# Gated linear attention ahead of two MLPs: the attention of chunks 9 to 23 in 64x64 quadrants, one visit a chunk

## The chip, the cores and the metric

The kernel runs on one core of one Trainium2 chip, in a single launch. The metric is the device time of that core in microseconds (us), smaller is better. PE is the matmul engine, DVE the vector engine, ACT the scalar (activation) engine, POOL the general-purpose engine, SP the engine that issues most DMAs. Each engine works through its own list of instructions in order and waits on semaphores.

## The reference, cut to what matters

```python
def _attn_ref(q, k, v, alpha):            # batch 4, heads 8, seq 768, head_dim 48
    state = np.zeros((B, H, D, D), dtype=np.float32)
    for t in range(S):
        state = alpha[:, :, t, :, None] * state + np.einsum('bhd,bhe->bhde', k[:, :, t], v[:, :, t])
        y[:, :, t] = np.einsum('bhd,bhde->bhe', q[:, :, t], state)
# x: y as 3072 tokens x 384
# MLP 1: h = x @ w_in (384 x 2048); g = h * sigmoid(h); x = g @ w_out
# MLP 2: sigmoid(x @ w_gate) * (x @ w_val), both 384 x 1536; then @ w_out
```

Everything is float32 outside; the weights reach the kernel as 64-bit words that it converts.

## The kernel before

**Chunks.** The 3072 tokens are 24 chunks of 128 (`C`), six to a sequence. Eight heads are four pairs (`NP`); the two heads of a pair lie on partitions 0 to 47 and 64 to 111 (`j` = 0, 1). Inside a chunk the recurrence becomes matrix products: `prep` (L278) scans the decays forward (A) and backward (G) on DVE, multiplies the keys by G and the queries by A, and leaves the decay over the whole chunk in `AE`.

**A chunk's products.** `scores` (L310) transposes the keys (PE, L319) and forms, for each head, the 128x128 block of keys times queries (L323) in two PSUM banks. `scores_done` masks the block with the causal triangle on DVE (L334, one instruction of 1024 columns, into M), and copies the transposed keys on ACT. `results` (L341) multiplies values by M (L352), keys by values into the new part of the state (L368, `u`), and the old state by the queries (L373, into the same bank as the values' product). `state` (L382) adds `u` and multiplies by the decay on DVE (L388, L389). `y_out` copies the result on ACT and moves 16 rows of each head's half by DMA, since 3 x 128 partitions hold 8 x 48 rows; `x_out` rounds it to the high half and DVE forms the low half that MLP 1 needs.

**MLPs.** Tokens go in six blocks of 512. A float32 product is three fp32r matmuls of 128x128 weights by 512 columns (`mm3`, L565 to L567: high by low, high by high, low by high). A step is one block `b` and one 128-row slice `f` of the hidden layer: `mm_in` (9 matmuls), `act` on ACT and DVE, and `mm_out` (9 matmuls) for the slice of two steps earlier. A step is 18 matmuls on PE.

**Order.** It is written out by hand (`manual_schedule`). A lead does chunks 0 to 8, with `full` products one after the other (L722 to L741); it prepares chunk c+2 in pass c, so that chunk 9 is prepared there too. Then the steps of MLP 1 run: 28 of them (`mixed`) alternate blocks 0 and 1 and also convert weights (`Way.half`, on DVE, ACT and POOL: L479 to L522). The tables `SCORES`, `RESULTS` and `DECAYS` (L47 to L53) put the attention of chunks 9 to 23 into steps: place 0 is between `mm_in` and `mm_out`, place 1 behind `mm_out`, place 3 is preparation. So PE visits a chunk twice, once for the scores and once for the results. Block 0's sums occupy the PSUM group 0 until step (0, 15) is done; after that attention has this group. MLP 2 follows behind block 5.

**Queues.** SP issues in this order: after the scores of chunk c the keys and decays of chunk c+4 (`load_decays`), after its results the queries and values of c+4, then the row moves of `y_out`. Four places hold the chunks' q, k and alpha in turn. In the lead ACT issues half of the row moves.

```python
            h = early.pop((b, f), None) or mm_in(ps_h, "h", "in", b, f)
            tensor(i, 0)
            way = way1 if i < mixed else way2 if b == NB - 1 else None
            act(b, f, h, None, "out", way)
            others(i, 0)
            others(i, 3)
            if len(pend) > 2:
                mm_out()
            tensor(i, 1)
            others(i, 1)
```

Of the kernel before, what the change touches and what calls it, by code (L numbers as in the profile page):

```python
# [7 lines left out]
F32 = mybir.dt.float32  # L8
# [6 lines left out]
ALU = mybir.AluOpType  # L15
# [16 lines left out]
QW = 3 * NP * C  # L32
N = 512
# [148 lines left out]
def gated_attention_then_mlps(ctx: ExitStack, tc: tile.TileContext, qka, a0, v, w_in, w_out, w_gate, w_val, w_out2, out):  # L182
# [25 lines left out]
    causal = ap.tile([P, C], F32, name="causal")  # L208

    W = ap.tile([DP, NP * D + 16], F32, name="state")  # L210
    W_all = W[:, : NP * D].rearrange("r (p d) -> r p d", d=D)
# [31 lines left out]
    def constants():  # L243
# [5 lines left out]
        nc.gpsimd.affine_select(out=causal, in_=causal, compare_op=ALU.is_ge, fill=0.0, base=0, pattern=[[1, C]], channel_multiplier=-1)  # L249
        nc.vector.memset(dg, 0.0)  # L250
# [4 lines left out]
        nc.gpsimd.memset(W, 0.0)  # L255
# [17 lines left out]
    def check(c, i):  # L273

        x = (Gt, At)[i].pop(c)
        nc.scalar.activation(x, x, AF.Square, accum_out=chk[:DP, c, i : i + 1])

    def prep(c, step, p0=0, p1=NP, mul=None):  # L278
# [5 lines left out]
        if step == 0:  # L284
            if p0 == 0:
                Gt[c] = G_at[c % 2]
                At[c] = ap.tile([DP, NP * C], F32, tag="A", name="A", bufs=2)
# [11 lines left out]
        elif step == 1:  # L299
            nc.vector.tensor_tensor_scan(At[c][:, lo:hi], t[:, A_OFF + lo : A_OFF + hi], d1[:, lo:hi], 0.0, op0=ALU.mult, op1=ALU.add)  # L300
        else:
            q = t[:, lo:hi]
            mul.tensor_tensor(q, q, At[c][:, lo:hi], op=ALU.mult)

    S, T, M, KT, U, Y = {}, {}, {}, {}, {}, {}
# [4 lines left out]
    def scores(c, g, apart, p0=0, p1=NP):  # L310

        t = qk[c]
        if p0 == 0:
            S[c] = two_banks(g)
            if not last_of(c):
                T[c] = ps_h.tile([P, N], F32, tag="h", name="t") if apart else bank(g)
# [14 lines left out]
    def scores_done(c):  # L331
        for_all = causal.rearrange("s (j i t) -> s j i t", j=1, i=1).to_broadcast([P, 2, NP, C])
        M[c] = ap.tile([P, 2, NP, C], F32, tag="m", name="m", bufs=2)
        nc.vector.tensor_tensor(M[c], S[c].rearrange("s j (i t) -> s j i t", i=NP), for_all, op=ALU.mult)  # L334
# [6 lines left out]
    def results(c, g):  # L341
# [6 lines left out]
        for p in range(NP):  # L348
            for j, n in ((0, 64), (1, D)):
# [3 lines left out]
                    y[r : r + n, p * C : (p + 1) * C], v_c[:, h : h + n], M[c][:, j, p], start=p == 0, stop=first, skip_group_check=True  # L353
                )
        s = S.pop(c)
        if not last_of(c):
            u = ps_h.tile([P, N], F32, tag="h", name="u")[:DP] if c < LEAD else s[:DP, 0]
            U[c] = u[:, : NP * D]
            kt = KT.pop(c)
            sums = c < LEAD and not first  # L360
            if sums:
                for j, n in ((0, 64), (1, D)):
                    r = 64 * j
                    nc.tensor.matmul(u[r : r + n, : NP * D], ident[r : r + D, r : r + n], W[r : r + D, : NP * D], start=True, stop=False, skip_group_check=True)
            for p in range(NP):
                for j, n in ((0, 64), (1, D)):
                    r = 64 * j
                    nc.tensor.matmul(u[r : r + n, p * D : (p + 1) * D], kt[:, p, r : r + n], vt[c][:, 2 * p + j], start=not sums, stop=True, skip_group_check=True)  # L368
        if not first:
            for p in range(NP):  # L370
                for j, n in ((0, 64), (1, D)):
# [3 lines left out]
                        W[r : r + D, p * D : p * D + n],  # L375
# [6 lines left out]
    def state(c):  # L382

        u, w = U.pop(c), W[:, : NP * D]
        if c < LEAD or c % CB == 0:
            w = u
        else:
            nc.vector.tensor_tensor(w, u, w, op=ALU.add)  # L388
# [510 lines left out]
```

## Time and profile before

| | |
|---|---|
| Median of 3 runs | 976.45 us (974.56 to 976.94) |
| Profiled execution, its own time | 976.87 us |
| its span, first to last instruction | 974.8 us |
| mean granted TensorE clock | 0.987 |
| busy: PE, DVE, ACT, POOL | 98%, 46%, 39%, 10% |

A row of the timeline has the start in us from the span's start, the length in us, the engine and line, output<-inputs by the program's names, and how many instructions were merged (x16). In brackets stands idle time of the engine just before, and who ended it. Windows give busy time of each engine in a stretch. PE is the matmuls themselves, PEld the loading of their weights; matmuls are pipelined, so the distance of two starts, not the length of one, is what one costs. An fp32 matmul shows as two instructions.

### The profile page before, as it was taken

The numbers are of one execution on the slowest core, as the hardware profiler recorded it, in microseconds if no ns is written. First come the engines' busy times: TensorE is split into PE (matmuls) and PEld (weight loads), VectorE is DVE, ScalarE is ACT, GpSimd is POOL, SyncE is SP. The second block draws the span as 40 slices with busy tenths as digits, with TensorE's granted clock in tenths as the row PEclk, the third lists the DMA queues.
The fourth block names the chain that finished last, engine by engine and source line by source line (L and its number), as shares of the span: only waits on it lengthen the run. The fifth ranks groups of instructions, "written<-read, shape, count | busy, mean of one in ns | idle before, by whom it ended". The sixth has DMA issues, their size and how long they took to land.

```text
span 974.8 us, 12868 instructions
## 1 busy us (share of the span) xinstructions
PE 951.3 (98%) x5192; PEld 777.2 (80%) x5192; DVE 450.6 (46%) x640; ACT 381.9 (39%) x707; POOL 92.9 (10%) x105
## 2 busy tenths in 40 slices
PE   7879999999999999999999999999999999999997
PEld 5658887878888888888888888888888888888885
DVE  8777778644543434342766444443232222222221
ACT  3446666443334334333666344433222222221211
POOL 2223323100000000000221111110000000000000
PEclk8899999999999999999999999999999999999999
DMA  9753332130111210003332112001000000000001
GB/s 229 210 150 117 129 100 80 40 107 28 58 42 37 70 38 13 5 1 102 98 98 67 63 65 65 33 1 42 24 1 0 33 1 1 33 1 0 33 1 37
DMA packets 35348, 54.84 MB, mean 56 GB/s; under 512 B 3856, under 2 KB 24368, under 8 KB 35280
## 3 DMA queue, kind: packets, MB, share of 16 engines
q1 hardware_dynamic: 34512, 53.37, 17.9%
q8 instruction: 43, 0.70, 0.3%
q10 hardware_dynamic: 768, 0.56, 0.2%
q14 instruction: 25, 0.20, 0.1%
HBM read 48.02 MB, written 4.72 MB: 54 GB/s over the span
## 4 chain that ended last, share of the span: by engine, by line
PE 89%; DVE 3%; DMA 2%; ACT 2%; issue 1%; POOL 1%; SPq 0%; ACTq 0%; DVEq 0%
PE h L565 13%; PE h L567 13%; PE h L566 13%; PE s L565 6%; PE s L567 5%; PE s L566 5%; PE o L567 3%; PE o L565 3%; PE o L566 3%; PE v L565 3%; PE v L566 3%; PE v L567 3%; PE y L565 3%; PE y L567 3%; PE y L566 3%; PE s L323 2%
## 5 line engine op out<-in xcount | busy, mean ns | idle before, releaser
L565 PE MATMUL h<-x,w 128*128 128x512 f32 x582 | 228.0, 392 | 3.1 <-ACT w L504 1.7
L567 PE MATMUL h<-x,w 128*128 128x512 f32 x582 | 227.0, 390 | 0.8 <-POOL w L522 0.8
L566 PE MATMUL h<-x,w 128*128 128x512 f32 x582 | 227.0, 390 | 0.0
L593 DVE TENSOR_TENSOR gl<-g,gh 128x512 fp32r<-128x512 f32 x168 | 115.9, 690 | 194.9 <-ACT gh L592 194.2
L592 ACT ACTIVATE gh<-g 128x512 fp32r<-128x512 f32 x168 | 106.2, 632 | 157.0 <-DVE g L587 153.9
L565 PEld LDWEIGHTS h<-x,w 128*128 128x128 f32 x582 | 109.2, 188 | 28.0 <-ACT w L504 2.1
L567 PEld LDWEIGHTS h<-x,w 128*128 128x128 f32 x582 | 109.3, 188 | 25.0 <-POOL w L522 1.7
L566 PEld LDWEIGHTS h<-x,w 128*128 128x128 f32 x582 | 109.2, 188 | 22.8
L584 ACT ACTIVATE g<-h 128x512 f32<-128x512 f32 x96 | 57.0, 593 | 154.8 <-PE h L567 154.8
L587 DVE TENSOR_TENSOR g<-v,g 128x512 f32<-128x512 f32 x46 | 31.8, 692 | 178.7 <-PE v L567 178.7
L565 PE MATMUL s<-gl,w 128*128 128x512 f32 x240 | 96.5, 402 | 0.0
L586 ACT ACTIVATE g<-h 128x512 f32<-128x512 f32 x72 | 42.9, 596 | 132.6 <-PE h L567 132.6
L567 PE MATMUL s<-gh,w 128*128 128x512 f32 x240 | 93.7, 390 | 0.0
L566 PE MATMUL s<-gh,w 128*128 128x512 f32 x240 | 93.6, 390 | 0.0
L565 PE MATMUL o<-gl,w 128*128 128x512 f32 x144 | 56.1, 390 | 0.0
L567 PE MATMUL o<-gh,w 128*128 128x512 f32 x144 | 56.1, 390 | 0.0
L566 PE MATMUL o<-gh,w 128*128 128x512 f32 x144 | 56.1, 389 | 0.0
L522 POOL TENSOR_TENSOR w<-tmp,w 128x384 fp32r<-128x384 f32 x36 | 36.4, 1030 | 195.0 <-ACT w L504 195.0
L565 PEld LDWEIGHTS s<-gl,w 128*128 128x128 f32 x240 | 45.0, 187 | 12.4 <-issue 1.4
L587 DVE TENSOR_TENSOR g<-h,g 128x512 f32<-128x512 f32 x26 | 18.0, 692 | 79.3 <-PE h L567 79.3
L565 PE MATMUL v<-x,w 128*128 128x512 f32 x138 | 53.9, 391 | 0.0
L566 PE MATMUL v<-x,w 128*128 128x512 f32 x138 | 53.8, 390 | 0.0
(120 smaller groups left out, 1280.8 us busy)
## 6 DMA issues: line engine op xcount, KB each, us to landing
x<-in_moe_w_in SPq DMA_DIRECT2D x16, 384.0 KB, 3.6
x<-in_moe_w_out SPq DMA_DIRECT2D x16, 384.0 KB, 4.1
x<-in_qka SPq DMA_DIRECT2D x12, 448.0 KB, 4.2
qk<-in_qka SPq DMA_DIRECT2D x11, 448.0 KB, 3.7
v<-in_v SPq DMA_DIRECT2D x24, 192.0 KB, 3.1
raw<-in_moe_w_gate SPq DMA_DIRECT2D x12, 384.0 KB, 3.5
raw<-in_moe_w_val SPq DMA_DIRECT2D x12, 384.0 KB, 3.8
raw<-in_moe_w_out SPq DMA_DIRECT2D x12, 384.0 KB, 3.7
```

Source lines behind the costliest of these rows:

```text
L323: nc.tensor.matmul(S[c][:, j, p * C : (p + 1) * C], t[r : r + D, NP * C + p * C : NP * C + (p + 1) * C], t[r : r + D, p * C : (p + 1) * C] ...
L522: nc.gpsimd.tensor_tensor(l, b[:, i * SW : (i + 1) * SW].bitcast(F32), h.bitcast(F32), op=ALU.subtract)
L565: nc.tensor.matmul(ps, wh, x_l, start=first, stop=False)
L566: nc.tensor.matmul(ps, wh, x_h, start=False, stop=False)
L567: nc.tensor.matmul(ps, wl, x_h, start=False, stop=last)
L584: nc.scalar.activation(g, h, AF.Silu)
L586: nc.scalar.activation(g, h, AF.Sigmoid)
L587: nc.vector.tensor_tensor(g, val, g, op=ALU.mult)
L592: nc.scalar.activation(gh, g, AF.Copy)
L593: nc.vector.tensor_tensor(gl, g, gh.bitcast(F32), op=ALU.subtract)
```

## The change

For chunks 9 to 23 a chunk's 128 tokens are cut into two halves of 64 (`HC`). Only the two diagonal 64x64 blocks of the scores are formed; what the second half needs of the first goes through a state between them, so each chunk has two states (`W[c % 2][:, 0]` and `[:, 1]`). Every product uses 64 rows and up to 64 columns of the array: scores go to row half `j`, column half `h`; sums and values to row half `h`; the state's products to row half `j`, with the second half's outputs swapped (`j ^ h`). Bank `h` of one PSUM pair holds the results and the sums of half `h`. A `drain` of PE stands ahead of the state's products.

A chunk has one visit: transposes of chunk c+2, sums of c+1, values of c, scores of c+1, state's products of c. The tables `VISIT`, `G_AT` and `A_AT` place visits and preparation; chunk 9 is prepared in steps (0, 5) and (1, 5) and no longer in the lead. In the lead the mask multiply is two instructions of 512 columns, and M lies in weight buffers not yet in use. `tensor(i, 0)` is written behind `act`; the order of PE's own instructions stays. Last chunks of a sequence now have transposes and the sums of their first half. Left out below: renamed functions (`full_...`: the lead's), constants, and one-line tile changes.

```diff
-SCORES = {9: (1, 12, 0), 10: (1, 13, 0), 11: (1, 14, 0), 12: (1, 15, 2)}
-RESULTS = {9: (1, 12, 1), 10: (1, 13, 1), 11: (1, 14, 1), 12: (2, 2, 0)}
-
-DECAYS = {10: ((1, 9), (1, 10)), 11: ((1, 12), (1, 12)), 12: ((1, 14), (1, 14))}
-for _c in range(13, NC):
-    SCORES[_c] = (_c // 4 - 1, (0, 4, 8, 11)[_c % 4], 0)
-    RESULTS[_c] = (_c // 4 - 1, (2, 6, 10, 13)[_c % 4], 0)
+FIRST = {"T": (1, 11, 0), "scores": (1, 12, 0)}
+VISIT = {9: (1, 12, 1), 10: (1, 13, 0), 11: (1, 14, 0)}
+X_AT = {9: (1, 14)}
+G_AT = {9: (0, 5), 10: (0, 10), 11: (1, 9), 12: (1, 11), 13: (1, 13)}
+A_AT = {9: (1, 5), 10: (1, 8), 11: (1, 10), 12: (1, 12)}
+for _c in range(12, NC):
+    VISIT[_c] = (_c // 4 - 1, (2, 6, 10, 13)[_c % 4], 0)
...
+    def scores(c, p0=0, p1=NP):
+        t = qk[c]
+        if p0 == 0:
+            S[c] = bank(0), ps_h.tile([P, N], F32, tag="h", name="s")
+        for p in range(p0, p1):
+            for h in range(2):
+                for j in range(2):
+                    r, o = 64 * j, p * C + h * HC
+                    nc.tensor.matmul(
+                        S[c][j][h * HC : (h + 1) * HC, p * HC : (p + 1) * HC],
+                        t[r : r + D, K_OFF + o : K_OFF + o + HC],
+                        t[r : r + D, o : o + HC],
+                        start=True,
+                        stop=True,
+                    )
+    def scores_done(c):
+        for_all = causal2.rearrange("s (i t) -> s i t", i=1).to_broadcast([P, NP, HC])
+        M[c] = ap.tile([P, 2, NP, HC], F32, tag="m", name="m", bufs=2)
+        for j, s in enumerate(S.pop(c)):
+            nc.vector.tensor_tensor(M[c][:, j], s[:, :UA].rearrange("s (i t) -> s i t", i=NP), for_all, op=ALU.mult)
+        check(c, 1)
...
+    def open_results(c, g):
+        YU[c] = two_banks(g), set()
...
+    def sums(c):
+        yu, _ = YU[c]
+        kt = KT.pop(c + 1)
+        for p in range(NP):
+            for h in range(2):
+                for j, n in ((0, 64), (1, D)):
+                    r, o = 64 * j, UA + p * D
+                    if h == 0 or not last_of(c + 1):
+                        nc.tensor.matmul(
+                            yu[r : r + n, h, o : o + D],
+                            kt[h * HC : (h + 1) * HC, p, r : r + n],
+                            vt[c + 1][h * HC : (h + 1) * HC, 2 * p + j],
+                            start=started(c, h, j),
+                            stop=True,
+                            skip_group_check=True,
+                        )
+    def values(c):
+        yu, _ = YU[c]
+        v_c = vt[c].rearrange("t h e -> t (h e)")
+        for p in range(NP):
+            for h in range(2):
+                for j in range(2):
+                    to = j ^ h
+                    r, n, o = 64 * to, D if h or j else 64, (2 * p + j) * D
+                    nc.tensor.matmul(
+                        yu[r : r + n, h, p * HC : (p + 1) * HC],
+                        v_c[h * HC : (h + 1) * HC, o : o + n],
+                        M[c][h * HC : (h + 1) * HC, j, p],
+                        start=started(c, h, to),
+                        stop=first_of(c) and h == 0,
+                        skip_group_check=True,
+                    )
+    def queries(c):
+        yu, _ = YU[c]
+        w = W[c % 2]
+        nc.tensor.drain()
+        for p in range(NP):
+            for h in range(1 if first_of(c) else 0, 2):
+                for j in range(2):
+                    r, to, n = 64 * j, 64 * (j ^ h), D if h or j else 64
+                    nc.tensor.matmul(
+                        yu[to : to + n, h, p * HC : (p + 1) * HC],
+                        w[r : r + D, h, p * D : p * D + n],
+                        qk[c][r : r + D, p * C + h * HC : p * C + (h + 1) * HC],
+                        start=False,
+                        stop=True,
+                        skip_group_check=True,
+                    )
+    def state(c):
+        u = [YU[c - 1][0][:DP, h, UA : UA + NP * D] for h in range(2)]
+        wa, wb = (W[c % 2][:, h, : NP * D] for h in range(2))
+        if first_of(c):
+            nc.vector.tensor_copy(wb, u[0])
+        else:
+            nc.vector.tensor_tensor(wb, u[0], wa, op=ALU.add)
+        if not last_of(c):
+            nc.vector.tensor_tensor(W[(c + 1) % 2][:, 0, : NP * D], u[1], wb, op=ALU.add)
+            if c + 1 in AE:
+                decay(c + 1)
+    def decay(c):
+        w = W[c % 2][:, 0, : NP * D].rearrange("r (p d) -> r p d", d=D)
+        nc.vector.tensor_tensor(w, w, AE[c].rearrange("r (p d) -> r p d", d=1).to_broadcast([DP, NP, D]), op=ALU.mult)
...
+    def full_scores_done(c):
+        for_all = causal.rearrange("s (i t) -> s i t", i=1).to_broadcast([P, NP, C])
+        M[c] = M_lead[c % 2]
+        for j in range(2):
+            nc.vector.tensor_tensor(M[c][j], S[c][:, j].rearrange("s (i t) -> s i t", i=NP), for_all, op=ALU.mult)
...
+        w = W_lead[:, : NP * D]
+        if c + 1 == LEAD:
+            nc.vector.tensor_copy(w, U.pop(c))
         else:
-            nc.vector.tensor_tensor(w, u, w, op=ALU.add)
-        nc.vector.tensor_tensor(W_all, w.rearrange("r (p d) -> r p d", d=D), AE[c + 1].rearrange("r (p d) -> r p d", d=1).to_broadcast([DP, NP, D]), op=ALU.mult)
+            u, w = (x.rearrange("r (p d) -> r p d", d=D) for x in (U.pop(c), w))
+            nc.vector.tensor_tensor(w, u, AE[c + 1].rearrange("r (p d) -> r p d", d=1).to_broadcast([DP, NP, D]), op=ALU.mult)
...
+            y_halves(c, x, o)
...
-                    (nc.scalar if j and c < LEAD else nc.sync).dma_start(out=x[r + D : r + 64, i], in_=x3[r + 16 * i : r + 16 * (i + 1)])
+                    by = nc.scalar if j and (c < LEAD or c == LEAD + 2) else nc.sync
+                    by.dma_start(out=x[r + D : r + 64, i], in_=x[r + 16 * i : r + 16 * (i + 1), NK])
...
+    def y_halves(c, x, o):
+        yu = YU.pop(c)[0][:, :, :UA].rearrange("r h (p t) -> r h p t", p=NP)
+        nc.scalar.activation(x[:DP, :, o, :HC], yu[:DP, 0], AF.Copy)
+        for j in range(2):
+            r, at = 64 * j, 64 * (1 - j)
+            nc.scalar.activation(x[r : r + D, :, o, HC:], yu[at : at + D, 1], AF.Copy)
...
+        def visit(c):
+            open_results(c, 0)
+            if c + 2 < NC:
+                keys(c + 2)
+            if c + 1 < NC:
+                sums(c)
+            values(c)
+            if c + 1 < NC:
+                scores(c + 1)
+                queries(c)
+        def visited(c):
+            if c + 5 < NC:
+                load_decays(c + 5)
             if c + 4 < NC:
                 load_queries(c + 4)
                 load_values(c + 4)
...
-            if c + 2 <= LEAD:
+            if c + 2 < LEAD:
                 for s in range(3):
                     prep(c + 2, s)
...
-            for c, (b, f, end) in SCORES.items():
-                put(at[b, f], end, "scores", c)
-                if c > LEAD:
-                    first, then = (at[x] for x in DECAYS[c]) if c in DECAYS else (at[b, f] - 3, at[b, f] - 2)
-                    put(first, 3, "prep0", c)
-                    put(then, 3, "prep1", c)
-            for c, (b, f, end) in RESULTS.items():
-                put(at[b, f], end, "results", c)
-                put(at[b, f] + 1, 1, "x_out", c)
+            b, f, end = FIRST["T"]
+            put(at[b, f], end, "keys", LEAD)
+            b, f, end = FIRST["scores"]
+            put(at[b, f], end, "keys", LEAD + 1)
+            put(at[b, f], end, "first", LEAD)
+            for c, x in G_AT.items():
+                put(at[x], 3, "G", c)
+            for c, x in A_AT.items():
+                put(at[x], 3, "A", c)
+            for c, (b, f, end) in VISIT.items():
+                i = at[b, f]
+                if c > 11:
+                    if c + 1 < NC:
+                        put(i - 3, 3, "A", c + 1)
+                    if c + 2 < NC:
+                        put(i - 2, 3, "G", c + 2)
+                put(i, end, "visit", c)
+                if c + 1 == NC:
+                    put(i, 1, "queries", c)
+                put(at[X_AT[c]] if c in X_AT else i + 1, 1, "x_out", c)
...
+                elif what == "first":
                     scores_done(c)
-                elif what == "results":
-                    results_done(c)
+                    state(c)
+                    YU.pop(c - 1)
+                    load_decays(c + 4)
+                elif what == "visit":
+                    if c + 2 < NC:
+                        keys_done(c + 2)
+                    if c + 1 < NC:
+                        scores_done(c + 1)
+                        state(c + 1)
+                        visited(c)
+                        y_out(c)
+                elif what == "queries":
+                    y_out(c)
...
-                elif what == "prep0":
+                elif what == "G":
+                    check(c - 1, 1)
                     prep(c, 0)
-                    states()
-                elif what == "prep1":
+                    if c == LEAD:
+                        decay(c)
+                elif what == "A":
+                    check(c, 0)
                     prep(c, 1)
                     prep(c, 2)
...
-            tensor(i, 0)
             way = way1 if i < mixed else way2 if b == NB - 1 else None
             act(b, f, h, None, "out", way)
+            tensor(i, 0)
```

## Rows read from the trace of the kernel before

**Rows 1.** The page, busy time by engine and the chain that ended last
```profile
PE 951.3 (98%) x5192; PEld 777.2 (80%) x5192; DVE 450.6 (46%) x640; ACT 381.9 (39%) x707; POOL 92.9 (10%) x105
...
PE 89%; DVE 3%; DMA 2%; ACT 2%; issue 1%; POOL 1%; SPq 0%; ACTq 0%; DVEq 0%
```

**Rows 2.** Windows: stretch, its us, busy us of each engine, granted clock, DMA
```profile
100.00:150.00 50.00, 50.00 (x222) 41.19 (x221) 37.80 (x48) 32.77 (x54) 15.68 (x16) 1.00 0.36 119
300.00:450.00 150.00, 150.00 (x995) 122.61 (x994) 61.62 (x87) 56.90 (x118) 4.23 (x6) 1.00 0.09 24
```

**Rows 3.** Timeline of PE, a scores visit: start us, us, instruction, [idle before]
```profile
294.12 0.39 PE L567 MATMUL h<-x,w 128*128 128x512 f32 x1
294.35 0.55 PE L319 MATMUL y<-ident,qk 112*128 112x112 f32 x4
294.83 1.16 PE L323 MATMUL s<-qk 48*128 48x128 f32 x16
295.92 0.50 PE L565 MATMUL s<-gl,w 128*128 128x512 f32 x1
296.25 0.39 PE L566 MATMUL s<-gh,w 128*128 128x512 f32 x1
```

**Rows 4.** Timeline of PE, a results visit
```profile
304.00 0.39 PE L567 MATMUL h<-x,w 128*128 128x512 f32 x1
304.32 1.09 PE L352 MATMUL y<-m,v 128*64 128x128 f32 x16
305.24 0.62 PE L368 MATMUL s<-v,kt 128*48 128x48 f32 x16
305.79 1.08 PE L373 MATMUL y<-qk,state 48*64 48x128 f32 x16
306.80 0.50 PE L565 MATMUL s<-gl,w 128*128 128x512 f32 x1
307.14 0.39 PE L566 MATMUL s<-gh,w 128*128 128x512 f32 x1
```

**Rows 5.** Timeline of PE, ten nanoseconds of the scores visit
```profile
294.83 0.38 PE L323 MATMUL s<-qk 48*128 48x128 f32 x2
```

**Rows 6.** Lines of PE kept apart by shape, the end of the sums (305.764 to 305.768)
```profile
L368 PE MATMUL s<-v,kt 128*64 128x48 f32 x2 | 0.3, 222 | 0.0
```

**Rows 7.** Timeline of weight loads that began after idle time put down to issue
```profile
7.45 0.23 PEld L319 LDWEIGHTS t<-ident,qk 112*128 112x128 f32 x1 [0.62 <-issue]
...
61.21 0.19 PEld L565 LDWEIGHTS h<-x,w 128*128 128x128 f32 x1 [0.17 <-issue]
```

**Rows 8.** Timeline of all engines, chunk 9 prepared in the lead
```profile
55.03 0.34 DVE L389 TENSOR_TENSOR state<-u,aend 112x192 f32<-112x192 f32 x1
...
55.30 1.21 DVE L292 TENSOR_TENSOR_SCAN G<-qk,dg 112x511 f32<-112x511 f32 x1
...
55.45 1.55 PE L323 MATMUL s<-qk 48*128 48x128 f32 x16 [1.92 <-POOL qk L303]
...
59.02 0.69 DVE L303 TENSOR_TENSOR qk<-qk,A 112x512 f32<-112x512 f32 x1
...
59.63 1.22 DVE L334 TENSOR_TENSOR m<-s,causal 128x1024 f32<-128x1024 f32 x1
...
63.50 1.09 PE L352 MATMUL y<-m,v 128*64 128x128 f32 x16
...
65.34 0.54 PE L364 MATMUL u<-state,ident 48*64 48x192 f32 x4 [0.75 <-DVE state L389]
```

**Rows 9.** Timeline of all engines, a scan among the conversions
```profile
167.37 1.22 DVE L292 TENSOR_TENSOR_SCAN G<-x,dg 112x511 f32<-112x511 f32 x1
...
167.49 3.59 POOL L522 TENSOR_TENSOR w<-x,w 128x384 fp32r<-128x384 f32 x2 [4.78 <-ACT w L504]
...
168.56 0.39 PE L566 MATMUL h<-x,w 128*128 128x512 f32 x1
...
169.43 0.50 PE L567 MATMUL h<-x,w 128*128 128x512 f32 x1 [0.48 <-POOL w L522]
```

More of the change, by code (lines that the diff above doesn't have):

```diff
@@ L32 @@
 QW = 3 * NP * C
+HC = C // 2
+UA = NP * HC
 N = 512
@@ L208, in gated_attention_then_mlps @@
     causal = ap.tile([P, C], F32, name="causal")
-    W = ap.tile([DP, NP * D + 16], F32, name="state")
-    W_all = W[:, : NP * D].rearrange("r (p d) -> r p d", d=D)
+    causal2 = ap.tile([P, HC], F32, name="causal2")
+    W = [ap.tile([DP, 2, NP * D + 16], F32, name=f"state{i}") for i in range(2)]
+    W_lead = W[LEAD % 2][:, 0]
     d1 = ap.tile([DP, NP * C], F32, name="d1")
@@ L303, in prep, with first_of @@
             mul.tensor_tensor(q, q, At[c][:, lo:hi], op=ALU.mult)
-    S, T, M, KT, U, Y = {}, {}, {}, {}, {}, {}
+    M_lead = [[wp.tile([P, 2, NK, P], F32R, tag="w", name="m2").bitcast(F32).rearrange("p a k c -> p (a k c)") for _ in range(2)] for _ in range(2)]
+    M_lead = [[x[:, : NP * C].rearrange("s (i t) -> s i t", i=NP) for x in m] for m in M_lead]
+    S, T, M, KT, YU, U, Y = {}, {}, {}, {}, {}, {}, {}
     def last_of(c):
         return c % CB == CB - 1
-    def scores(c, g, apart, p0=0, p1=NP):
+    def first_of(c):
+        return c % CB == 0
@@ new lines, in scores_done, with started @@
+    def scores_done(c):
[4 more added lines that the diff above has]
+        check(c, 1)
+    def started(c, h, col):
+        yu, begun = YU[c]
+        new = (h, col) not in begun
+        begun.add((h, col))
+        return new
@@ L367, in results @@
                     r = 64 * j
-                    nc.tensor.matmul(u[r : r + n, p * D : (p + 1) * D], kt[:, p, r : r + n], vt[c][:, 2 * p + j], start=not sums, stop=True, skip_group_check=True)
+                    nc.tensor.matmul(u[r : r + n, p * D : (p + 1) * D], kt[:, p, r : r + n], vt[c][:, 2 * p + j], start=not plus, stop=True, skip_group_check=True)
         if not first:
@@ L692, in gated_attention_then_mlps @@
         way1.load(0)
-        late = []
-        def states():
-            while late and (last_of(late[0]) or late[0] + 1 in AE):
-                c = late.pop(0)
-                if not last_of(c):
-                    state(c)
-        def results_done(c):
-            late.append(c)
-            if c >= LEAD - 1:
-                states()
+        def visit(c):
[11 more added lines that the diff above has]
+                load_decays(c + 5)
             if c + 4 < NC:
@@ L708, in results_done, with states @@
                 load_values(c + 4)
-            y_out(c)
-            if c == 0:
-                way1.load(1)
+        late = []
+        def states():
+            while late and (late[0] + 1 == LEAD or last_of(late[0]) or late[0] + 1 in AE):
+                c = late.pop(0)
+                if not last_of(c):
+                    full_state(c)
         for p0, p1 in ((0, 2), (2, NP)):
@@ L735, in gated_attention_then_mlps @@
                 early[0, 0] = mm_in(ps_h, "h", "in", 0, 0)
-            results(c, c % 2)
+            full_results(c, c % 2)
             if c == LEAD - 1:
                 x_out(c - 1)
-            results_done(c)
+            late.append(c)
+            if c == LEAD - 1:
+                states()
+            load_queries(c + 4)
+            load_values(c + 4)
+            y_out(c)
+            if c == 0:
+                way1.load(1)
             for _ in range(CONV.get(c, 0)):
```

99 lines of the change are left out of this document (59 added, 40 removed).

## The prediction

> **What bounds the kernel now.** The page first: PE is busy 98% of the span, and the chain that ended last is 89% PE [rows 1]. The windows then say where: from 100 to 150 us, where weights are converted, and from 300 to 450, PE alone is busy throughout, at granted clock 1.00 (its upper level, 2.4 GHz), while DVE and ACT are at 76% and 66%, then at 41% and 38% [rows 2]; only in the lead does DVE go from one instruction to the next without a gap [rows 8]. So after the lead the time is the sum of PE's own instructions; what the other engines do counts only when PE waits.
>
> The PE timeline shows what attention costs there. Steady MLP matmuls start 0.227 us apart. A scores visit (4 transposes, 16 score instructions) puts 2.13 us between the last matmul ahead of it and the second behind it, so it costs 2.13 - 2 x 0.227 = 1.68 us [rows 3]. A results visit (values, sums, state) costs 3.14 - 0.454 = 2.69 us [rows 4]. Inside them: transposes 0.48 us, of which 0.09 is the change of array shape (304.00 to 304.32 is 0.32 instead of 0.227); values 0.92, sums 0.55 with the change behind them, state products with the way out 1.01; on the way out two starts are some 0.10 late each. Chunks 9 to 23: 12 scores visits at 1.68, 3 without transposes (last of a sequence) at 1.68 - 0.39 = 1.29; 10 full results visits at 2.69, 3 without sums at 2.69 - 0.46 = 2.23, 2 without state products at 2.69 - 1.01 = 1.68. Sum 20.2 + 3.9 + 26.9 + 6.7 + 3.4 = **61.0 us**, all on the path.
>
> **The change, part by part.**
>
> *PE.* Each fp32 matmul is two instructions. Scores: 8 matmuls of 48x128 weights by 128 columns become 16 of 64-column weights by 64 columns, a fourth of the array each; half of each 128x128 block, which the mask zeroes, isn't computed. Values and state products go the same way, sums split in two 64-row halves with 48 columns as before. Every section is now 32 instructions, 8 on each of four quadrants. Do four run side by side? The trace shows the two halves of it: two row halves start scores in the same 10 ns (x2) [rows 5], and two column halves share the 16 sums [rows 4, 6]. Those 16, with 64 or 48 weight columns and 48 moving ones, take 305.24 to 305.79 less the 0.09: 0.46 us, 8 in turn on each half, 57 ns each. A quadrant's instruction also has 64 or 48 weight columns, and 64 moving columns (half of the 0.115 us that 128 take in values): again about 57 ns. So a section of four quadrants costs 8 x 0.057 = 0.46 us, if nothing but the quadrant limits it. Bounds from both sides: 0.43 (only the 64 moving columns), 0.90 (32 instructions at the densest rate that the trace shows, 0.46/16 = 28 ns). I take 0.46, the nearest row.
>
> *The drain* ahead of the state products is new, and the trace has no such thing inside the run. Behind it in PE's queue stand the state products, then mm_out and the next mm_in, all of which wait. It waits for the last scores to leave the array: a matmul of this size takes 0.22 us from start to end [rows 6], 0.16 more than its turn. Then PE's queue has to deliver anew: idle times put down to "issue" were 0.17 and 0.62 us [rows 7]. So 0.16 to 0.8; I take 0.40 with the first weight load in it, nearer to the 0.17, which fell in the same stage of fast matmuls; the 0.62 was at the start of the run.
>
> *A full visit:* transposes and change of shape 0.48, first weights 0.05, sums, values, scores 3 x 0.46, drain 0.40, state products 0.46, way out 0.20 = **2.97 us**, where two visits cost 1.68 + 2.69 = 4.37. There are 13 (chunks 9 to 21): 38.6. Chunk 22 has no transposes: 2.58. Chunk 23: values alone 0.80, state products alone 1.15. Ahead of it all: transposes of chunk 9 alone 0.39; transposes, sums, scores at (1,12) 0.48 + 0.05 + 0.92 + 0.20 = 1.65. Sum 45.2. **PE gains 61.0 - 45.2 = 15.8 us.**
>
> *DVE.* The mask multiply shrinks from 1024 to 2 x 256 columns; the state gets a third small operation (0.34 us [rows 8]). Both lie under PE, which is busy throughout while DVE has 59% free [rows 2]. If that cover went, the third operation would cost 15 x 0.34 = 5 us; the visits are 2.5 steps (10 us) apart, so it doesn't, except at chunks 9, 10 and 11, which follow each other after one step or half of one. There M and the state have 2 us of mm_out. In them DVE has one 512-column subtraction, two mask multiplies of 256 and three state operations, some 2.5 us by 0.69 and 0.34 [rows 8], of which the subtraction lies ahead. I count 0.3 us for the bank of block 0, whose copy now stands behind the scan for chunk 12.
>
> *Preparation moved.* The scans and multiplies of chunk 9 leave the lead: five operations, 4.4 us of DVE from 55.30 to 59.7 [rows 8]. What ended the lead's waits there was not DVE: scores of chunk 8 waited for POOL's multiply until 55.45, then PE shows no idle time until 63.50, while M of chunk 8, next on DVE, was done at 60.9. PE's wait at 65.34 is for a state that DVE reached late, while it waited for ACT. So the removal gives 0 (bounds: 0, and -4.4 if it were all on the path). Against it the mask multiply of the lead is split in two, 2 x 0.69 (the 512-column L303) for 1.22 [rows 8]: +0.16 nine times, of which the two or three shortly ahead of 55 us, where DVE has no gap, count: +0.35 (bounds 0 and 1.4).
> In the conversion stretch DVE gets the scans of 9 and 10 and half of 11 and 12 earlier: some 10 us more in 105 us that had 24% free [rows 2]. The trace has one such insertion: the scan of chunk 10 at 167.37 beside POOL's two weight halves, which took 3.59 us together, and PE waited: 169.43 instead of 168.56 + 0.227, and 0.11 on the start behind it, 0.75 us in all [rows 9]. That one stays (now chunk 11). Four are new, at (0,5), (1,5), (0,10), (1,8). PE idles nowhere from 100 to 150 us [rows 2], so there the conversions have some room: I count a third of 4 x 0.75, 1.0 us (bounds 0 and 3.0).
>
> *Queues.* load_decays comes after a visit for chunk c+5, not after the scores for c+4; its landing lies under two visits (20 us). ACT issues three of chunk 11's row moves, from an engine 38% busy there [rows 2]. The row moves and loads otherwise keep their order. POOL clears a second state and mask while DVE and DMA hold the lead. All 0.
>
> **Sum** against the profiled execution (976.87, span 974.8): -15.8 + 0.3 + 0.35 + 1.0 = -14.1, 962.7; the median is 0.4 lower, so **962 us**.
>
> A rule that speaks against it: the Trainium skill, "TensorE: Matmul & The Clock Gate", section "Wait — 56ns, not 53.3ns?", has matmul starts never closer than about 25 ns however small they are. By it, as an estimate, a section would take 0.80 us and the sum 983. The rows show two starts within 10 ns [rows 5], but no run of many below 28 ns [rows 4], so they don't decide.
> Another: "TensorEngine Tiling (Array Packing)", "Gotcha 1: PSUM Pressure", says that different row tiles cannot use one PSUM bank at once; here both row halves of the state products write one bank. By it that section would double and the sum be about 969. The trace disagrees for two tiles: L373 writes one bank from both row halves, 16 in 1.01 us, no slower than L323 with a bank for each, 1.09 [rows 3, 4].
>
> **Rivals.**
> *1, slower: PE cannot feed four quadrants.* Place: every section. If 28 ns per instruction, the densest that the rows show, is PE's rate of issue and not the weight load's, a section costs 0.85 to 0.90 and 60 sections (13 x 4 + 2 + 4 + 2) give back 60 x 0.39 = 23.4 us or more: **986**. It decides from 0.695 us a section, 21.7 ns an instruction. For it: the 16 sums follow 16 slower instructions, so what PE holds ready ahead may have fed them; no row shows a faster rate that lasts. Against: if issue set the pace, the 48- and 64-column halves would finish together, but the last two running are both 64 wide [rows 6]; and starts within 10 ns exist. A rate between (18 ns) gives 969 to 970.
> *2: the gain comes, part is given back in waits:* each new scan among the conversions costs the 0.75 of [rows 9] (+2.0), and visits 9 to 11 wait for DVE (M, state, scan of the next: up to 2.5): **967**.
> *3: quadrants collide in PSUM:* the state products run two at a time: 15 x 0.46 = 6.9: **969**.
> *4: the lead gets shorter* because DVE was full there: up to 4 us: **958**.
>
> **How the numbers follow.** Forecast 0.55, rival 4 0.07, rival 2 0.12, rival 3 0.04, rival 1 half way 0.08, in full 0.14. The forecast's own range is 956 to 967 (section 0.43 to 0.50, drain 0.16 to 0.6). Over all: 955 to 976, which leaves out rival 1 in full and a little below. A measurement tells 0.3% (2.9 us) from no change: faster 0.79, same 0.05, slower 0.16.
>
> **What would show it.** Right: a visit of some 2.9 to 3.1 us between MLP matmuls, 32 starts in 0.46 us, granted clock still 1.00. Rival 1: quadrant sections of 0.8 us. Drain: the gap ahead of the state products. Rival 2: PE idle times put down to DVE, POOL or ACT between 100 and 200 us. Lead: first steady MLP matmul at 73.75 plus 0.3. Wrong at the root: two quadrants in turn instead of four.

## The result, and the profile after

The changed kernel takes **967.44 us** (median of 4 runs, 967.12 to 967.84) against 976.4: ratio 0.9912, 95% interval 0.9895 to 0.9929. The forecast was 962.0, so it is faster, and 5.4 us less so than forecast. The profiled execution took 967.63 us (span 965.9), the one before 976.87 (974.8); the ledger below is made between these two, and explains the 8.9 us by which the spans differ.

The page after, for [rows 1]: PE has lost 19 us of busy time and some of its share of the chain; DVE now has 6% of it instead of 3%, "issue" 4% instead of 1%, ACT and POOL as much as before.

```profile
PE 932.2 (97%) x6164; PEld 763.2 (79%) x6164; DVE 451.5 (47%) x682; ACT 391.1 (40%) x725; POOL 96.1 (10%) x109
...
PE 84%; DVE 6%; issue 4%; ACT 2%; DMA 2%; POOL 1%; SPq 0%; ACTq 0%; DVEq 0%; POOLq 0%
```

The windows after, for [rows 2]: the later stretch is as full of PE's work as it was, bar the drains and one wait of 0.32 us; the conversion stretch is not. There PE was busy for all of 50 us, and now idles for 2 of them, while DVE and POOL have more work.

```profile
100.00:150.00 50.00, 48.02 (x207) 37.92 (x206) 40.94 (x54) 31.17 (x54) 16.01 (x15) 1.00 0.34 111
300.00:450.00 150.00, 148.32 (x1498) 122.22 (x1497) 57.86 (x95) 63.62 (x129) 3.52 (x5) 1.00 0.11 29
```

**The visit**, PE's timeline after (a row is start, length, instruction, count), where [rows 3, 4] were two visits:

```profile
279.60 0.39 PE L719 MATMUL h<-x,w 128*128 128x512 f32 x1
279.83 0.55 PE L336 MATMUL t<-ident,qk 112*128 112x112 f32 x4
280.31 0.62 PE L386 MATMUL s<-v,kt 64*64 64x48 f32 x30
...
281.58 0.22 PE L352 MATMUL y<-qk 48*64 48x64 f32 x2
281.59 0.25 PE L352 MATMUL s<-qk 48*64 48x64 f32 x2
281.64 0.22 PE L352 MATMUL y<-qk 48*64 48x64 f32 x2
281.65 0.25 PE L352 MATMUL s<-qk 48*64 48x64 f32 x2
281.70 0.22 PE L352 MATMUL y<-qk 48*64 48x64 f32 x1
282.10 0.67 PE L423 MATMUL s<-x,state 48*64 48x64 f32 x32 [0.18 <-issue]
282.70 0.50 PE L717 MATMUL s<-gl,w 128*128 128x512 f32 x1
283.04 0.40 PE L718 MATMUL s<-gh,w 128*128 128x512 f32 x1
```

Four instructions start per 58 ns, as one on each quadrant gives: the two `y` at 281.58 within 5 ns, of the two `s` at 281.59 the second 31 ns behind the first (the row is 0.25 us long, each of them 0.22), and the next four 58 ns later. From the first sum to the last score are 281.70 - 280.31 = 1.39 us for three sections of 32. The drain is the gap from 281.70 to 282.10. The whole visit costs 283.04 - 279.60 less two spacings of 0.227, some 2.98 us; the 13 full visits cost 2.96 to 2.99.

**The lead** got 2.6 us shorter: the first MLP matmul, which started at 61.21 together with the load of its weights [rows 7], starts at 58.65. Where it arises, in the timeline before (two rows that no step of the prediction had used):

```profile
32.85 0.28 ACT L406 ACTIVATE x<-y 112x128 f32<-112x128 f32 x1 [5.15 <-DMA x<-x]
...
39.38 0.88 PE L364 MATMUL u<-state,ident 48*64 48x192 f32 x4 [4.04 <-DVE state L389]
```

and in the timeline after:

```profile
32.64 0.66 ACT L548 ACTIVATE x<-y 112x128 f32<-112x128 f32 x2 [0.49 <-PE y L513]
...
36.83 0.53 PE L504 MATMUL u<-state,ident 48*64 48x192 f32 x4 [1.75 <-DVE state L529]
...
58.65 0.50 PE L717 MATMUL h<-x,w 128*128 128x512 f32 x1
```

ACT's copy of a chunk's outputs waited 5.15 us for a DMA, the row moves of the pair of chunks before, which read the single buffer `x3`. The changed `y_out` copies those rows into a fourth slot of `x`, which has two buffers (one of the tile changes that the diff leaves out); the copy waits 0.49 us, for PE.

**The conversion stretch** lost 6.9 us: the MLP matmul that started at 179.34 starts at 183.95, 4.61 later, after 2.56 earlier at the end of the lead; 0.32 of these 7.17 us are the transposes of chunk 9, which now stand right ahead of it and belong to attention. The timeline after, around the G scan of chunk 9, and the later stalls:

```profile
106.10 0.96 DVE L633 SCALAR_TENSOR_TENSOR x<-x 128x768 uint32<-128x768 uint32 x1
...
107.58 1.22 DVE L302 TENSOR_TENSOR_SCAN G<-qk,dg 112x511 f32<-112x511 f32 x1
...
109.96 0.55 DVE L664 TENSOR_SCALAR x<-x 128x768 uint16<-128x768 uint16 x1
...
112.78 0.50 PE L717 MATMUL h<-x,w 128*128 128x512 f32 x1 [1.10 <-ACT w L656]
113.87 0.50 PE L719 MATMUL h<-x,w 128*128 128x512 f32 x1 [0.36 <-POOL w L674]
...
135.40 0.50 PE L719 MATMUL h<-x,w 128*128 128x512 f32 x1 [0.36 <-POOL w L674]
...
158.06 0.50 PE L717 MATMUL h<-x,w 128*128 128x512 f32 x1 [1.95 <-ACT g L736]
...
159.51 0.63 PE L719 MATMUL h<-x,w 128*128 128x512 f32 x1
159.94 0.63 PE L717 MATMUL h<-x,w 128*128 128x512 f32 x1
...
173.71 0.50 PE L719 MATMUL h<-x,w 128*128 128x512 f32 x1 [1.02 <-POOL w L674]
```

Between two steps of one weight's conversion (L633 and L664) DVE does chunk 9's scan and product and a state's decay, 107.58 to 109.96. The weight is late, and PE waits for ACT's half of it, then for POOL's. At 158 us PE waits for ACT's Silu, which stands in ACT's order behind a late half. A stall is here what the starts lose against the steady spacing of 0.227 us: those at 113, 135, 158 and 174 us cost 2.0, 1.1, 2.2 and 1.3 us. Behind the third the granted clock falls to its lower level, 1.2 GHz: eight matmuls start 0.43 us apart, 1.6 us more. In the windows (columns as in [rows 2]):

```profile
155.00:158.00 3.00, 1.11 (x5) 0.57 (x4) 1.21 (x2) 2.20 (x4) 1.60 (x2) 1.00 0.77 262
158.00:162.50 4.50, 4.44 (x12) 3.49 (x13) 4.43 (x6) 3.28 (x7) 0.36 (x1) 0.62 0.16 32
```

Together 8.2, less 1.6 that the kernel before had lost itself in that stretch (the 0.75 of [rows 9] and 0.84 around 157 us): 6.6 of the 6.9.

**The start of a pass** is new too. Timeline after:

```profile
214.71 1.22 DVE L312 TENSOR_TENSOR_SCAN A<-qk,d 112x512 f32<-112x512 f32 x1
215.96 0.69 DVE L315 TENSOR_TENSOR qk<-qk,A 112x512 f32<-112x512 f32 x1
216.56 0.95 DVE L575 TENSOR_TENSOR x<-x,x 128x768 fp32r<-128x768 f32 x1
...
217.66 0.47 PE L717 MATMUL h<-x,w 128*128 128x512 f32 x1 [1.86 <-DVE x L575]
```

The next block's x waits in DVE's order behind chunk 13's A scan, and PE waits for x: 2.1 us. A later pass starts 0.6 late, at 446 us; no scan stands ahead of its x, for which DVE itself had waited 3.40 us for ACT.

**Ledger**, added from the PE timelines: lead -2.6, conversions +6.9, attention 61.0 to 45.55 = -15.4, pass starts +2.7, small changes of spacing -0.5: -8.9.

### The profile page after: what moved, and what is told of

It is laid out like the page before. It is cut to its first block, busy times and chain, and to the rows that moved or that the text cites. A ratio compares the mean times of both kernels' runs of the same rounds, so it can differ in the third digit from the quotient of the medians.

```text
span 965.9 us, 14889 instructions
## 1 busy us (share of the span) xinstructions
PE 932.2 (97%) x6164; PEld 763.2 (79%) x6164; DVE 451.5 (47%) x682; ACT 391.1 (40%) x725; POOL 96.1 (10%) x109
## 4 chain that ended last, share of the span: by engine, by line
PE 84%; DVE 6%; issue 4%; ACT 2%; DMA 2%; POOL 1%; SPq 0%; ACTq 0%; DVEq 0%; POOLq 0%
PE h L717 12%; PE h L719 12%; PE h L718 12%; PE s L717 5%; PE s L718 4%; PE s L719 4%; PE o L719 3%; PE o L717 3%; PE o L718 3%; PE v L717 3%; PE v L718 3%; PE v L719 3%; PE y L717 2%; PE y L719 2%; PE y L718 2%
## 5 line engine op out<-in xcount | busy, mean ns | idle before, releaser
L717 PE MATMUL v<-x,w 128*128 128x512 f32 x138 | 53.9, 391 | 0.0
L718 PE MATMUL v<-x,w 128*128 128x512 f32 x138 | 53.8, 390 | 0.0
L719 PE MATMUL v<-x,w 128*128 128x512 f32 x138 | 53.7, 389 | 0.0
```

What stands on the lines that cost most here:

```text
L717: nc.tensor.matmul(ps, wh, x_l, start=first, stop=False)
L718: nc.tensor.matmul(ps, wh, x_h, start=False, stop=False)
L719: nc.tensor.matmul(ps, wl, x_h, start=False, stop=last)
```

## The experiments

Ratios are to the kernel before on the same chip, with 95% intervals. The lead alone ends between 57.3 and 59.7 us in the profiled executions of all kernels with two buffers, so one execution says nothing about less than a us or so there. Nor is the clock the same in all of them: in the traces of all experiments but six it is at its lower level for a part of 70 to 77 us, which costs some 1.5 us, and in before, after and six it isn't. Experiment two's window there (after has 1.00 in place of the 0.76):

```profile
70.00:77.00 7.00, 6.69 (x23) 5.44 (x24) 5.38 (x7) 5.25 (x9) 2.23 (x4) 0.76 0.43 147
```

So traces are compared here by single waits, and the kernels by the medians and ratios of all their executions.

**One: the second buffer alone**, in the kernel before.

```diff
-            xf[m] = ap.tile([P, NK, 2, C], ...), ap.tile([DP, 2, C], F32, tag="x3", name="x3")
+            x3 = x3_odd if m in (1, 3) else ap.tile([DP, 2, C], F32, tag="x3", name="x3")
+            xf[m] = ap.tile([P, NK, 2, C], ...), x3
```

> The kernel before, with one thing of the change taken alone: the rows of the fourth slot (x3) get a second tile, so that the row moves of the next pair no longer wait for a pair's outputs. In the trace of before, ScalarE's copy at 32.85 us ends an idle stretch of 5.15 us on a DMA into x, and TensorE waits 4.04 us at 39.38 us; in the trace after, TensorE's wait there is 1.75 us and the lead ends 2.56 us sooner. Theory (the lead's gain is the second buffer of the moved rows): about 2.6 us faster than before, near 974, with the first MLP matmul at about 58.7 us instead of 61.2. Rival (the lead's gain comes from chunk 9's preparation having left it): same as before within 0.5 us, 976.4, and the idle stretch of TensorE at 39 us stays at 4 us.

974.59 us, ratio 0.9971 (0.9958 to 0.9984). Its timeline: the copy no longer waits, PE's wait is halved, and the first MLP matmul starts at 58.29.

```profile
32.96 0.26 ACT L409 ACTIVATE x3o<-y 112x128 f32<-112x128 f32 x1
...
36.53 0.53 PE L364 MATMUL u<-state,ident 48*64 48x192 f32 x4 [1.93 <-DVE state L389]
...
58.29 0.50 PE L568 MATMUL h<-x,w 128*128 128x512 f32 x1
```

The theory holds: 0.9971 is 2.8 us, the interval 1.6 to 4.1 (by the medians 1.8), and the copy's wait is gone. The size isn't the lead's alone: in this trace PE is 3.1 us ahead of the kernel before at 66 us, loses 1.6 to the lower clock, and wins 1.0 because it waits less between 155 and 170 us.

**Two: chunk 9 back in the lead.**

```diff
-G_AT = {9: (0, 5), 10: (0, 10), 11: (1, 9), 12: (1, 11), 13: (1, 13)}
-A_AT = {9: (1, 5), 10: (1, 8), 11: (1, 10), 12: (1, 12)}
+G_AT = {10: (0, 10), 11: (1, 9), 12: (1, 11), 13: (1, 13)}
+A_AT = {10: (1, 8), 11: (1, 10), 12: (1, 12)}
...
-            if c + 2 < LEAD:
+            if c + 2 <= LEAD:
```

> The changed kernel with one part undone: chunk 9 is prepared in the lead again (its G scan and its A scan), and not among the MLP steps; quadrants and the rest stay. Theory (the lead's gain is not chunk 9's, and its preparation among the MLP steps is what makes the conversions wait): the lead stays as short as after (first MLP matmul at 58.7 to 59.2 us), and TensorE's stalls at 112.8 and 113.9 us (about 2.0 us together) and a part of those at 134 and 135 us (1.1 us) go, so 2 to 3 us faster than after: 964.5 to 965.5. Rival (the lead became short because chunk 9 left it): the lead is 2.6 us longer again, and the total 967 to 967.5, no change.

963.56 us, ratio 0.9863 (0.9843 to 0.9883). The first MLP matmul starts at 57.89: the lead carries chunk 9's 4.4 us of DVE at no visible cost, so its absence is not what made the lead short.

```profile
57.89 0.50 PE L717 MATMUL h<-x,w 128*128 128x512 f32 x1
```

The windows from 110 to 150 us, after and here:

```profile
110.00:150.00 40.00, 38.02 (x163) 29.64 (x162) 32.80 (x43) 24.29 (x43) 13.31 (x12) 1.00 0.34 115
```

```profile
110.00:150.00 40.00, 40.00 (x178) 33.14 (x177) 31.19 (x41) 25.58 (x43) 12.83 (x13) 1.00 0.31 108
```

Less DVE work, and PE full again. The gain of 3.9 us by the medians is larger than the 2 to 3 expected; in the traces the stall at 158 us shrank as well (to 0.6 us of idle time, without the half-clock spell). That conversions which are late once stay late, so that chunk 10's scan met them with less in hand, is my reading of this and no experiment of its own.

**Three: chunk 13's A scan one step later.**

```diff
-                        put(i - 3, 3, "A", c + 1)
+                        put(i - 3 + (c == 12), 3, "A", c + 1)
```

> The changed kernel with one scan moved: the A scan of chunk 13 runs four MLP steps later, at the start of the next pass, behind the output of chunk 11 in VectorE's order rather than ahead of it. In the trace after, TensorE's first MLP matmul of that pass waits 1.86 us for an x that VectorE writes at 216.56 us behind the scan (214.71 us, 1.22 us) and its product (215.96 us, 0.69 us). Theory (the scan is what the wait at the pass's start is made of): 1.5 to 2.1 us faster than after, near 965.5, and that stall under 0.4 us. Rival (the wait is the output's own chain, or moves to chunk 12's visit, which needs the scan): within 0.5 us of after, 967.4.

966.17 us, ratio 0.9884 (0.9864 to 0.9904): by the medians 1.3 faster, though the intervals overlap. (The edit moves the scan by one step, not by the four of which the expectation speaks.) The timeline decides: the wait went, and part came back in the visit behind, where the scans delayed DVE's copy of block outputs, by it ACT's Silu, and by that the bank for the scores. That visit cost 3.85 us instead of 2.96.

```profile
218.15 0.47 PE L717 MATMUL h<-x,w 128*128 128x512 f32 x1 [0.17 <-DVE x L575]
...
228.76 0.27 PE L352 MATMUL s<-qk 48*64 48x64 f32 x1 [0.58 <-ACT g L736]
```

Theory and rival each held in part.

**Four: quadrants in pairs.** The same in sums, values and queries as in scores:

```diff
-        for p in range(p0, p1):
-            for h in range(2):
+        for h in range(2):
+            for p in range(p0, p1):
```

> The changed kernel with the order of its quadrant matmuls turned: in scores, sums, values and queries the loop over the two halves of the rows is the outer one, over the pairs of heads the inner one, so that of four matmuls in a row two at a time use different quarters of the array rather than four. The number of matmuls, their sizes, the state between and the one visit stay the same. Theory (a section is short because four quadrants work side by side): each of the two sections of 32 goes from 0.46 to about 0.92 us, a visit from 2.98 to some 4.8 us, and the fifteen chunks cost about 25 us more: near 992, over the kernel before. Rival (the gain comes from half the score area and from one visit in place of two, whatever the order): 967 to 969.

979.85 us, ratio 1.0035 (1.0019 to 1.005): slower than the kernel before. A visit costs 3.87 us, 0.89 more, half of what was expected. The timeline of its scores and state products:

```profile
287.91 0.22 PE L352 MATMUL s<-qk 48*64 48x64 f32 x1
287.92 0.22 PE L352 MATMUL y<-qk 48*64 48x64 f32 x1
287.97 0.22 PE L352 MATMUL s<-qk 48*64 48x64 f32 x1
287.98 0.22 PE L352 MATMUL y<-qk 48*64 48x64 f32 x1
...
288.92 0.94 PE L423 MATMUL s<-x,state 48*64 48x64 f32 x32
```

Two start per 58 ns where it was four. First to last start, scores double as expected, 0.49 to 0.92 us; sums, values and state products only go from 0.46, 0.52 and 0.45 to 0.72, 0.73 and 0.73, since the end of one half still overlaps the start of the other. Even so the order of two loops is worth 12.4 us, more than the whole gain of the change: the rival falls, and the theory's size with it.

**Five: chunk 9 in the lead, and chunk 13's A scan in its old step, but behind the output of chunk 11.**

```diff
-                        put(i - 3, 3, "A", c + 1)
+                        put(i - 3, 1 if c == 12 else 3, "A", c + 1)
```

> The kernel with chunk 9 prepared in the lead again, and one thing more: the A scan of chunk 13 stands behind the output of chunk 11 in VectorE's order of the same MLP step, rather than ahead of it. (One step later, as tried, it took the wait at the start of the pass away, 1.9 to 0.2 us, but pushed the copies of the block's outputs back, and a visit waited 0.9 us for them.) Theory (that wait is only the order of two pieces of work on VectorE): the wait at the start of the pass under 0.4 us, no new one in the visit behind it, and 1.3 to 1.7 us faster than with chunk 9 in the lead alone (963.6): about 962. Rival (whichever place the scan has there, it delays something as long): within 0.5 us of 963.6.

962.14 us, ratio 0.9849 (0.9833 to 0.9866); the interval overlaps that of two, so the trace decides. From 208 to 216 us PE is busy for all 8.00 us; the wait at the start of the pass, 1.41 us with chunk 9 in the lead, is gone, and its visit has no new one. As the theory had it.

**Six: chunk 11's scans one step later**, on top of five. Its A scan then reads chunk 12's reciprocals, here and in seven, so both compute wrong results for chunk 11: they show what the order of the work costs and are no versions to use.

```diff
-G_AT = {10: (0, 10), 11: (1, 9), 12: (1, 11), 13: (1, 13)}
-A_AT = {10: (1, 8), 11: (1, 10), 12: (1, 12)}
+G_AT = {10: (0, 10), 11: (1, 10), 12: (1, 11), 13: (1, 13)}
+A_AT = {10: (1, 8), 11: (1, 11), 12: (1, 12)}
```

> The same, and the scans of chunk 11 one step later each, so that the G scan falls behind the last weight conversion. With chunk 9 in the lead, the G scan at 167.33 us runs beside GpSimd's two weight halves, which take 3.58 us instead of 1.98, its product with the keys takes 1.21 us instead of 0.66, and TensorE's matmuls lose 1.5 us right behind. Theory (VectorE's scan and GpSimd's conversions slow each other, and a conversion comes late): GpSimd's last halves take 2.0 us, the 1.5 us at 167 us go, and it is 1.0 to 1.6 us faster than the run without it: 960.5 to 961. Rival (the stretch from there on has no room for two scans in one step, and the first visits wait for them): within 0.5 us.

963.91 us, ratio 0.9863 (0.9847 to 0.988): by the medians 1.8 slower than five, with overlapping intervals. The expected wait did go. In five's timeline, and then in six's:

```profile
167.85 3.58 POOL L674 TENSOR_TENSOR w<-x,w 128x384 fp32r<-128x384 f32 x2 [4.77 <-ACT w L656]
...
169.79 0.50 PE L719 MATMUL h<-x,w 128*128 128x512 f32 x1 [1.23 <-POOL w L674]
```

```profile
168.13 0.50 PE L719 MATMUL h<-x,w 128*128 128x512 f32 x1 [0.17 <-POOL w L674]
...
185.26 0.99 PE L386 MATMUL s<-v,kt 64*64 64x48 f32 x30 [2.16 <-ACT x L778]
```

But the sums of chunk 9 wait 2.16 us for ACT's copy of the first block's outputs, held up by DVE's half of that copy, which now stands behind chunk 12's G scan, chunk 11's A scan and their products. The rival's wait took its place. A wait of 1.96 us at 153 us, 0.37 in five's trace, and a half-clock spell behind it (granted clock 0.51 from 155 to 158) also fell into this profiled execution. PE had been 2.3 us ahead of five's from 74 to 150 us, by a shorter lead and the full clock at 70 to 77, and gave 1.6 of it back at that wait: what the lead wins, the conversions can take again, and the terms of the ledger aren't independent.

**Seven: six, with chunk 10's scans cut in two** (pairs of heads 0 and 1 in the old steps, 2 and 3 at (1, 7) and (0, 12)).

```diff
...
+                elif what == "G0":
+                    check(c - 1, 1)
+                    prep(c, 0, 0, 2)
+                elif what == "G1":
+                    prep(c, 0, 2, NP)
...
```

> The same, and the scans and products of chunk 10, the one chunk that is left among the conversions, each cut into two halves that stand in two steps (VectorE's total work there rises slightly). Theory (what delays a conversion is the length of one uninterrupted insertion on VectorE, 1.9 to 2.1 us, against gaps of 1.2 us between its steps): of the 1.3 us that this chunk costs there at least 0.7 go: 0.7 to 1.3 us faster than the run without it. Rival (the conversions are held up by VectorE's total work, not by the length of a piece): no change within 0.4 us, or slightly slower.

963.45 us, ratio 0.9855 (0.9839 to 0.9872), 0.5 by the medians: not told apart by the time. PE has no wait left at 153 or 160 us, but the sums still wait 2.19.

**Eight: five, with only chunk 11's G scan a step later.**

```diff
-G_AT = {10: (0, 10), 11: (1, 9), 12: (1, 11), 13: (1, 13)}
+G_AT = {10: (0, 10), 11: (1, 10), 12: (1, 11), 13: (1, 13)}
```

> The kernel with chunk 9 in the lead and chunk 13's A scan behind chunk 11's output (962.1 us), and the G scan of chunk 11 one step later, its A scan left where it was, so that both fall between the last weight conversion and the copies of the first block's outputs. With the A scan moved on too, those copies (VectorE's, then ScalarE's) came 2 us late and the first sums of the quadrant chunks waited 2.16 us for them, while the 1.2 us that TensorE had waited for GpSimd's weights at 168 us shrank to 0.2; that run also gave chunk 11 the reciprocals of chunk 12, since the scans there overwrote them, and its results for that chunk are others. Theory (both were VectorE's order alone): no wait over 0.4 us at 168 nor at 185 us, 1.0 to 1.6 us faster: 960.5 to 961.1. Rival (there is no room for both in one step either): within 0.5 us of 962.1.

961.31 us, ratio 0.9849 (0.9835 to 0.9863), no different from five by the ratio.

```profile
167.00 2.10 POOL L674 TENSOR_TENSOR w<-x,w 128x384 fp32r<-128x384 f32 x2 [4.77 <-ACT w L656]
...
168.06 0.50 PE L719 MATMUL h<-x,w 128*128 128x512 f32 x1 [0.35 <-POOL w L674]
...
183.87 0.68 PE L386 MATMUL s<-v,kt 64*64 64x48 f32 x32 [0.84 <-ACT x L778]
```

POOL's two halves take 2.10 us without the scan beside them, 3.58 with it, and 0.9 us of PE's wait go; 0.5 come back at the sums (0.84 against 0.31 in five). Between theory and rival.

**Nine: eight, with chunk 10's scans cut in two** as in seven.

> The same with chunk 10's scans and products cut into halves in two steps each, the cut that took the waits at 154 and 161 us away (0.55 us of TensorE's idle time from 150 to 163 us) in a run in which the first sums waited 2 us for the copies. Theory (the length of one uninterrupted insertion on VectorE delays the conversions): 0.4 to 0.8 us faster than the run beside it without the cut, 960.0 to 960.6. Rival (total work): no change within 0.3 us.

960.62 us, ratio 0.9842 (0.9828 to 0.9855): 0.7 by the medians, not resolved by the ratios. Windows of eight, then nine:

```profile
150.00:163.00 13.00, 12.44 (x52) 9.30 (x52) 9.75 (x12) 8.32 (x15) 3.97 (x4) 1.00 0.28 92
```

```profile
150.00:163.00 13.00, 12.96 (x56) 10.06 (x55) 10.89 (x15) 8.32 (x15) 5.00 (x4) 1.00 0.30 92
```

PE regains 0.52 us although DVE does 1.1 us more: in that trace it is the length of one piece that delays a conversion, not the sum. It has the lowest time of all versions, by its ratio 15.4 us (1.6%) under the kernel before, but isn't told apart from eight.

## Why the prediction was right and wrong

The 967.4 lies in the range over all (955 to 976) and just outside the forecast's own (956 to 967). The mechanism on PE was right; the terms for the lead and the conversions were not, one for the start of a pass was missing, and the errors partly cancel.

**PE: right, step by step.** Visit 2.97 predicted, 2.98 measured; chunk 22 2.58 and 2.59; chunk 23 0.80 + 1.15 and 0.81 + 0.95; first transposes 0.39 and 0.40; total 45.2 and 45.55. The section of 0.46 followed from one row of a nearby case, the 16 sums on two column halves. Rival 1 is refuted by the timeline (32 starts in 0.45 to 0.52 us), and experiment four shows what two quadrants at a time cost. The rule of starts 25 ns apart, of "TensorE: Matmul & The Clock Gate" in the Trainium skill, section "Wait — 56ns, not 53.3ns?", does not hold for quadrants here: four per 58 ns are 14.5 each. Rival 3 falls: the 32 state products, from both row halves into one bank for each half of the tokens, started within 0.45 us. So the rule that row tiles cannot use one bank at once, of "TensorEngine Tiling (Array Packing)" in the Trainium skill, "Gotcha 1: PSUM Pressure", does not show here either.

**The drain: right**, 0.40 taken between bounds of 0.16 and 0.8, and 0.40 measured; that it fits so closely is luck. No run leaves the drain out.

**The bank of block 0: right**, 0.3 predicted, 0.32 measured. Visits 9 to 11 wait for nothing else. The 10 us between visits are those of the kernel before; after they lie 15 to 23 us apart from chunk 12 on, which only gives DVE more room. Timeline after:

```profile
189.03 0.68 PE L386 MATMUL s<-v,kt 64*64 64x48 f32 x32 [0.32 <-ACT x L778]
```

**The lead: wrong, +0.35 predicted, -2.6 measured.** The step that failed is "The row moves and loads otherwise keep their order. ... All 0." The order stayed, but the buffer did not: I checked what is queued behind what, not which copy waits for which transfer to release its tile. ACT's idle 5.15 us "<-DMA" stood in the trace. That chunk 9's leaving gives 0 was right; experiments one and two show it from both sides, to a us or so; the 0.35 for the mask multiply can't be seen within that. Rival 4 had the sign, by a cause that was not there.

**The conversions: wrong, +1.0 predicted, +6.9 measured**, outside the bounds of 0 to 3.0. The step that failed is "I count a third of 4 x 0.75". The 0.75 was what PE lost in one place by one insertion; it is not the price of one. The first three new insertions keep DVE for 2.4, 2.5 and 1.9 us, and the stalls behind them cost 2.0, 1.1 and 2.2; behind the fourth, chunk 10's A scan at 160.29 with PE at half clock, none is seen. So what an insertion costs is nearer to its own length, less what the conversions are ahead. That PE idled nowhere said that they were ahead, not by how much: at the first some 0.4 us, estimated as 2.4 less 2.0. I also took the one that stays at its old price: with POOL's halves beside the scan (3.6 against 2.0 us) it cost 0.75 before and 1.3 after. And I left out the half clock behind a stall, 1.6.

**The start of a pass: not in the sum, +2.7.** I followed what each scan delays among the conversions and the first visits, not the one that the new table puts ahead of a block's x. Five shows that the 2.1 at 217 us were order alone; the 0.6 at 446 us had no scan ahead of them, and their cause stays open.

So the 5.4 us between 962.0 and 967.4 are 5.9 and 2.7 too little for waits, against 2.9 too little for the lead and small terms. That the sum came so near is in part luck. Rival 2's 967 fits by number, and its kind of wait is the right one, but its visits 9 to 11 did not wait, and the waits among the conversions were more than twice its 3.0, hidden by a gain that it did not have.

What stays open: whether the half-clock spells come from the waits ahead of them. In the profiled executions they followed waits of some 2 us (158 us after, 153 and 185 us in six, 185 us in seven), but the 1.86 us at 217 us was followed by none. Three, with the same conversions as after, shows it best: its wait of 1.91 us at 158 us was followed by none (granted clock 1.00 from 158 to 162.5), its 1.23 us at 174 by one (0.53 from 175 to 178.6), and the same 1.23 us in five, at 170 us, by none. So the place of these 1.6 us in the ledger belongs to one execution, not to the kernel.

## What to carry to other kernels

Price an insertion on an in-order engine by its own length, less only so much as its consumers are shown to be ahead; a busy PE doesn't show how much that is. For every tile that a change gives another buffer or slot, look up who waits for its release. Where work runs in quarters of the array, write the loops so that four different quarters stand next to each other in the queue.

## What was not expected of the hardware

Matmuls of 48x64 or 64x64 weights by 64 columns start four per 58 ns on four quadrants, in a sustained run of 32, and two per 58 ns where four neighbours in the queue fall on two quadrants. POOL's weight halves, 128x384 each, take 3.58 us for two beside a DVE scan and product, 1.96 to 2.10 without; DVE's product of 112x512 beside them takes 1.21 instead of 0.66 us (in experiment two's timeline).
